# Attention, GLU and gate in one kernel: another order of the last two heads' query blocks, the first gate weights prepared among the projections, transposes two chunks at a time, and P times V at the end in twos

## The chip, the cores and the metric

The kernel runs on one core of a Trainium2 chip. A core has TensorE (PE in the profile, its weight loads PEld), VectorE (DVE), ScalarE (ACT), GpSimd (POOL) and SyncE (SP), each with an instruction queue that it works through in order, and 16 DMA engines. The metric is the device time of one execution in microseconds (us), the median of several runs. Before the change it is 2739.11 us (three runs, 2738.48 to 2739.22).

## The reference

With x of 2048 rows and 576 features, 32 heads of 18 features and a gate width of 4608:

```python
xn  = layernorm(x)
qkv = xn @ wqkv                                  # 576 -> 3 * 576
p   = softmax(q @ k^T * 18 ** -0.5)              # 32 heads, 2048 x 2048 each
s   = concat_heads(p @ v) @ wo
gate = xn @ W_gate;  gate = gate * (gate > 0)    # 576 -> 4608
h    = gate * (xn @ W_up)
g    = silu(h @ W_down)                          # 4608 -> 576
out  = x + s * g
```

Everything is float32.

## The kernel before

Almost every product is made of three float32r products: each operand is split into a rounded high part and the rest (low), and high x high, high x low and low x high are added up (`PRODUCTS`). `split_pool` (L96) makes such a pair on POOL, with a copy (L97) and a subtraction (L98); `split_full` (L89) makes one from PSUM, high on ACT (L90) and low on DVE (L91). All matmuls are issued at L64 and all transposes at L67, so the tile's name tells them apart.

**Projections.** The 2048 rows are taken in four groups g of 512. For each group `stats` and `normalize` work out the layernorm, and `transposed` turns the normalized rows into nine chunks of 64 features (`xs[g][c]`): four transposes into a PSUM bank (`tps`), then the split on ACT and DVE. For group 0 this is done ahead of all matmuls; for group g + 1 it is a generator (`rows_to_features`) that is fed into the matmuls of group g as `fill`: `row_pairs` issues the 54 matmuls of a block as 27 pairs (upper and lower 64 rows of the array at once) and takes one step of `fill` after every `every` pairs. `qk_block` makes 128 features of q and k at a time (four blocks, PSUM `pq`, then to DRAM as `qd`, `kd`), `qk_last` the rest, `v_block` makes v (PSUM `pv`, to DRAM as `vd`). In the last group the maxima for the first two heads (`pm`, reduced on DVE into `mx`, L189) are made among the matmuls of `v_block`.

**Units.** Then come 144 units, one for each of 36 slices of the gate width and four row groups. A unit k needs `gw`, the gate and up weights of its slice: `up_weights` loads them (`rg`) and splits them on POOL. It makes 54 matmuls (`pg`), relu and product (`h`, `hh`), and every second unit adds to `y` with 48 matmuls (`py`, `down`). Each unit begins by preparing the weights of unit k + 1; those of unit 0 are prepared by a call just before the first unit. Spread among the matmuls of units 9 to 143 lies the attention of 15 pairs of heads: scores (`psx`), exponentials on ACT (`p`, L640), P times V (`po`, `attend`), and the maxima of the next pair. The maxima reach the scores as extra rows of `qT`: `max_rows` works them out and writes them with eight small DMAs of SP (`qT<-nt`, L562) for two query blocks at a time. After the last slice of a row group `gate_steps` turns `y` into the silu factor, in pieces between matmuls: exponential on ACT (L508), plus one on DVE (L510), six reciprocals on DVE (L514), product on POOL (L515) and a store to `gd`.

**The end.** The 16th pair of heads (u = 15) is left for the end, with the output projection woven in. `exp_steps` with `last` takes the four query blocks of 512 in the order of `LASTQ`, each with 16 key tiles; two key tiles of both heads make one `p` tile and one `attend`. In the loop at the bottom each round issues four `psx`, takes at most one `attend`, and then about 2.2 us of matmuls from the generator `outputs`: the last `down`, then for each tile of 128 rows the output projection (`pw`) of its first 512 features (`first4`), whose heads come from DRAM (`od`, through `load_heads` and `heads`, tiles `o4`, `hf`), with the rows of `gd` and x (`rows_of`: `gt`, `xr`). The four tiles of `tail`, those of the last query block in `LASTQ`, get `first4` early and their last 64 features (`last1`, from `o5T`) at the very end. A query block is closed when `finish` has written its rows into `o5`. The weights `wo` are loaded and split on POOL when the units are over (`rw`, L739, L742).

What sets the order: the program's own text for matmuls, transposes and the operations marked `keep`; for the rest a scheduler that places each instruction on its engine's queue. SP issues nearly all loads, in its queue's order, and an SP entry that waits for a free buffer holds all behind it.

## Time and profile before

| | |
|---|---|
| median of three runs | 2739.11 us |
| the profiled execution's own time | 2731.45 us |
| its span, first to last instruction | 2729.7 us |
| PE busy | 2681.5 us (98%) |
| DVE, ACT, POOL busy | 1916.1, 1475.1, 1200.6 us |
| mean granted TensorE clock | 0.993 |
| 16 DMA engines | 92 GB/s over the span |

The page's parts on busy time tell that PE works nearly all the span; where it does not is seen in the views that list, for each instruction, how long its engine stood idle before it and what ended that (written in brackets as `[4.25 <-POOL gw L97]`, and summed in the view of waits). The view by stretches gives for each stretch its length, then for each engine its busy time and the number of instructions begun, then the granted TensorE clock (1.00 is full), the busy share of the DMA engines and the rate in GB/s. Rows of a timeline begin with the start and the length in us; a row can merge several instructions (`x4`). SPq and POOLq rows are DMAs being issued.

### The profile page before, as it was taken

How to read it: one execution, taken by the hardware profiler on the slowest of the kernel's cores; microseconds unless marked ns; L12 is line 12 of the kernel's file. 1: busy time of each engine (PE TensorE's matmuls, PEld its weight loads, DVE VectorE, ACT ScalarE, POOL GpSimd, SP SyncE). 2: the span in 40 equal slices, each digit the busy share in tenths (PEclk: the TensorE clock that was granted, in tenths of full speed). 3: DMA queues.
4: the chain of work that ended last, by engine and by line, in shares of the span. 5: the costliest groups of instructions: out<-in, count | busy, mean ns of one | idle time of the engine just before them, and what ended most of it. 6: DMA issues, size and time to landing. Idle time of an engine off the chain costs nothing.

```text
span 2729.7 us, 55255 instructions
## 1 busy us (share of the span) xinstructions
PE 2681.5 (98%) x22100; PEld 2013.2 (74%) x22100; DVE 1916.1 (70%) x3250; ACT 1475.1 (54%) x2686; POOL 1200.6 (44%) x929
## 2 busy tenths in 40 slices
PE   8998999999999999999999999999999999999898
PEld 6897777777777777777777777777777777777566
DVE  5426677777777777777777777777777777777452
ACT  3321356565656555555655555555556465656464
POOL 4225844444444444444444444444444444444322
PEclk9999999999999999999999999999999999999899
DMA  9744232232253222222342222222423222222244
GB/s 253 206 161 120 62 81 72 64 79 66 76 134 82 73 72 74 73 72 68 92 121 80 74 73 68 77 73 68 121 76 80 63 76 75 76 65 55 74 140 150
DMA packets 290368, 250.17 MB, mean 92 GB/s; under 512 B 60288, under 2 KB 232064, under 8 KB 290112
## 3 DMA queue, kind: packets, MB, share of 16 engines
q1 hardware_dynamic: 282048, 218.33, 30.5%
q0 software_dynamic: 8064, 28.32, 3.1%
q8 instruction: 175, 2.87, 0.4%
q14 instruction: 81, 0.66, 0.1%
HBM read 201.51 MB, written 44.53 MB: 90 GB/s over the span
## 4 chain that ended last, share of the span: by engine, by line
PE 94%; POOL 2%; ACT 1%; issue 1%; DVE 1%; DMA 1%; SPq 0%; DVEq 0%; POOLq 0%; ACTq 0%
PE pg L64 29%; PE py L64 17%; PE po L64 17%; PE pm L64 12%; PE psx L64 10%; PE pq L64 4%; PE pw L64 2%; PE pv L64 2%; PE tps L67 1%; PE tp L67 1%; POOL gw L98 0%; POOL y L491 0%; POOL dw L98 0%; ACT p L640 0%; DVE e L510 0%
## 5 line engine op out<-in xcount | busy, mean ns | idle before, releaser
L189 DVE TENSOR_REDUCE mx<-pm 128x1 f32<-128x512 f32 x2048 | 1359.4, 686 | 286.8 <-PE pm L64 167.2
L640 ACT ACTIVATE p<-psx 128x512 f32<-128x512 f32 x2048 | 1168.3, 598 | 576.0 <-PE psx L64 479.0
L64 PE MATMUL pg<-x,gw 64*128 64x512 f32 x7668 | 1370.6, 394 | 8.0 <-POOL gw L97 4.2
L64 PEld LDWEIGHTS pg<-x,gw 64*128 64x128 f32 x7668 | 1049.9, 186 | 125.2 <-POOL gw L97 4.6
L64 PE MATMUL psx<-qT,kT 56*128 56x512 f32 x2048 | 782.8, 399 | 14.3 <-DMA qT<-nt 10.5
L64 PE MATMUL pm<-kT,qT 54*128 54x512 f32 x2048 | 776.7, 405 | 0.3 <-ACT p L490 0.2
L64 PEld LDWEIGHTS py<-dw,hh 128*128 128x128 f32 x3456 | 461.8, 189 | 62.5 <-issue 61.3
L463 POOL TENSOR_TENSOR hh<-h,hh 128x512 fp32r<-128x512 f32 x144 | 184.7, 1282 | 733.5 <-ACT hh L462 690.8
L64 PE MATMUL py<-dw,hh 128*128 128x288 f32 x3456 | 480.0, 298 | 0.6 <-POOL hh L463 0.6
L64 PE MATMUL po<-p,va 128*32 128x512 f32 x4096 | 474.0, 596 | 0.0
L493 DVE TENSOR_TENSOR y<-py,y 128x288 f32<-128x288 f32 x520 | 237.9, 457 | 311.1 <-PE py L64 310.1
L64 PEld LDWEIGHTS pm<-kT,qT 54*128 54x128 f32 x2048 | 358.7, 185 | 121.1 <-issue 58.7
L64 PEld LDWEIGHTS psx<-qT,kT 56*128 56x128 f32 x2048 | 367.5, 186 | 62.3 <-DMA qT<-nt 11.3
L98 POOL TENSOR_TENSOR gw<-rg,gw 128x1152 fp32r<-128x1152 f32 x144 | 385.7, 2678 | 11.6
L64 PEld LDWEIGHTS po<-p,va 128*32 128x32 f32 x4096 | 115.8, 109 | 262.0 <-issue 256.5
L97 POOL CAST dw<-rd 128x576 fp32r<-128x576 f32 x144 | 95.6, 664 | 481.9 <-DMA rd<-in_B_W_down_dram 199.0
L98 POOL TENSOR_TENSOR dw<-rd,dw 128x576 fp32r<-128x576 f32 x144 | 205.8, 1429 | 11.6
L462 ACT ACTIVATE hh<-h 128x512 fp32r<-128x512 f32 x144 | 90.8, 630 | 169.3 <-DVE h L460 169.3
L97 POOL CAST gw<-rg 128x1152 fp32r<-128x1152 f32 x144 | 165.1, 1146 | 0.0
L64 PE MATMUL pq<-x,wqk 64*128 64x512 f32 x972 | 121.2, 397 | 0.0
L458 ACT ACTIVATE r<-pg 128x512 f32<-128x512 f32 x144 | 85.7, 595 | 63.2 <-PE pg L64 41.5
L556 ACT ACTIVATE nt<-tp 32x128 fp32r<-32x128 f32 x32 | 8.5, 266 | 193.3 <-PE tp L67 193.3
(88 smaller groups left out, 1203.3 us busy)
## 6 DMA issues: line engine op xcount, KB each, us to landing
rg<-in_B_W_gate_dram SPq DMA_DIRECT2D x144, 288.0 KB
rg<-in_B_W_up_dram SPq DMA_DIRECT2D x144, 288.0 KB
rd<-in_B_W_down_dram SPq DMA_DIRECT2D x144, 288.0 KB
x<-xTd SPq DMA_DIRECT2D x54, 256.0 KB
qT<-qd SPq DMA_DIRECT2D x384, 36.0 KB
kT<-kd SPq DMA_DIRECT2D x384, 36.0 KB
qd<-hh POOLq DMA_DIRECT2D x16, 512.0 KB, 4.0
kd<-hh POOLq DMA_DIRECT2D x16, 512.0 KB, 5.4
```

What stands on the lines that cost most here:

```text
L64: return tc.keep_in_program_order(nc.tensor.matmul(*args, **kw))
L67: return tc.keep_in_program_order(nc.tensor.transpose(*args))
L97: keep(nc.gpsimd.tensor_copy(hi, raw))
L98: keep(nc.gpsimd.tensor_tensor(lo, raw, hi.bitcast(F32), ALU.subtract))
L189: nc.vector.tensor_reduce(mx[:, g % 2, h, j, c : c + 1], ps, axis=AX.X, op=ALU.max)
L458: nc.scalar.activation(r, ps[0], AF.Relu)
L462: nc.scalar.activation(hh[:, 0], h, AF.Copy)
L463: keep(nc.gpsimd.tensor_tensor(hh[:, 1], h, hh[:, 0].bitcast(F32), ALU.subtract))
L493: nc.vector.tensor_tensor(ys[j][:, cs], ps, ys[j][:, cs], ALU.add)
L556: nc.scalar.activation(nt_.bitcast(F32R), ps[0:32, 0:P], AF.Copy)
L640: nc.scalar.activation(pts[key][:, h, i, :], ps, AF.Exp, scale=SCALE)
```

## The change

There are seven edits.

1. `transposed` yields after every second chunk instead of after each, and for groups 1 to 3 a step of `fill` is taken after every ninth pair of matmuls instead of every sixth.
2. For group 0 only the first four chunks (three steps) are transposed ahead of the matmuls; the others are taken in the first `qk_block`, a step after every sixth pair.
3. `up_weights(0)` is called after the last group's `qk_block`s and ahead of its `v_block`; `units`, `gus` and the function move up for that.
4. In `gate_steps` the addition of one goes from DVE to ACT.
5. `LASTQ` is (0, 3, 2, 1) instead of (3, 0, 2, 1): the query blocks counted from 1, in the order 1, 4, 3, 2.
6. In the loop at the bottom two `attend` are taken when three `p` tiles are ready, instead of one when two are.
7. The tail tiles' `gt` are kept in buffers of their own and not loaded again for the last step; their transposes from `o5` come after one row tile instead of two; of the last additions, those of tiles 0 and 2 are on POOL and those of 1 and 3 on DVE (before: 0 and 1 on POOL, 2 and 3 on DVE).

```diff
@@ -191,6 +191,19 @@
                         tasks.append((max_rows, ([qTs[u, g - 1], qT], mx)))
                     yield
 
+    units = [(g, f) for g in (NQ - 1, *range(NQ - 1)) for f in range(NF)]
+    gus = {}
+
+    def up_weights(k):
+        if k >= len(units):
+            return
+        f = units[k][1]
+        rg = wr.tile([P, KC, P], F32, name="rg")
+        load2(rg, [[(wg, f * P, P)], [(wu, f * P, P)]])
+        gw = ws.tile([P, 2, KC, P], F32R, name="gw")
+        split_pool(gw[:, 0], gw[:, 1], rg)
+        gus[k] = gw
+
 
     with ExitStack() as st:
         one = pool(st, "one", 1)
@@ -275,7 +288,8 @@
                 xs[g].append(xc)
                 if c % 3 == 0 and c + 3 < KC:
                     normalize(c + 3)
-                yield
+                if c % 2:
+                    yield
 
         def rows_to_features(g, xt):
             ln = []
@@ -304,10 +318,10 @@
                     fs = slice(f0, f0 + p1 - p0)
                     nc.gpsimd.dma_start(t[:, fs, gs].rearrange("i p s -> p i s"), hb[p0:p1])
 
-        def qk_block(b, gw, g, fill):
+        def qk_block(b, gw, g, fill, every):
             ps = next_pair("pq")
             row_pairs(
-                ps, lambda t, c, i, j, rows: (gw[rows, i, c, :], xs[g][c][rows, j, :]), fill
+                ps, lambda t, c, i, j, rows: (gw[rows, i, c, :], xs[g][c][rows, j, :]), fill, every
             )
             store_qk(b, ps, [(g, False), (g, False)])
 
@@ -360,8 +374,9 @@
             "wv", HC, [[[(wqkv, 2 * D + m * VH, VH)], [(wqkv, 2 * D + HC + m * VH, VH)]] for m in range(3)]
         )
         wqk.append(weights("wqk4", P, [[[(wqkv, C4, DT), (wqkv, D + C4, DT)]] * 2], pl=ws, tag="gw"))
-        for _ in transposed(0, *ln0):
-            pass
+        first = transposed(0, *ln0)
+        for _ in range(3):
+            next(first)
         for g in range(NQ):
             fill = None
             if g % 2:
@@ -376,7 +391,10 @@
             if g + 1 < NQ:
                 fill = rows_to_features(g + 1, nxt)
             for b in range(4):
-                qk_block(b, wqk[b], g, fill)
+                if b == 0 and g == 0:
+                    qk_block(b, wqk[b], g, first, 6)
+                else:
+                    qk_block(b, wqk[b], g, fill, 9)
                 if b == 0 and g == NQ - 1:
                     load_q(0, 0)
                     for c in range(NQ):
@@ -388,6 +406,8 @@
             if fill is not None:
                 for _ in fill:
                     pass
+            if g == NQ - 1:
+                up_weights(0)
             mx = [max_steps(0, h) for h in range(2)]
             v_block(wv, g, zip(*mx) if g == NQ - 1 else None)
 
@@ -398,20 +418,9 @@
     wl = pool(mid, "wl", 2, "right")
     yp = pool(mid, "yp", 8, "right")
 
-    units = [(g, f) for g in (NQ - 1, *range(NQ - 1)) for f in range(NF)]
-    gus, dws, hhs = {}, {}, {}
+    dws, hhs = {}, {}
     N1 = 9
     xcur = {NQ - 1: xs[NQ - 1]}
-
-    def up_weights(k):
-        if k >= len(units):
-            return
-        f = units[k][1]
-        rg = wr.tile([P, KC, P], F32, name="rg")
-        load2(rg, [[(wg, f * P, P)], [(wu, f * P, P)]])
-        gw = ws.tile([P, 2, KC, P], F32R, name="gw")
-        split_pool(gw[:, 0], gw[:, 1], rg)
-        gus[k] = gw
 
     def down_weights(k):
         f = units[k][1]
@@ -505,9 +514,9 @@
         while gates:
             y, t = gates.pop(0)
             e = wl.tile([P, D], F32, name="e", bufs=1)
-            tc.keep_in_program_order(nc.scalar.activation(e, y, AF.Exp, scale=-1.0))
+            keep(nc.scalar.activation(e, y, AF.Exp, scale=-1.0))
             yield
-            tc.keep_in_program_order(nc.vector.tensor_scalar(e, e, 1.0, None, op0=ALU.add))
+            keep(nc.scalar.activation(e, e, AF.Copy, bias=1.0))
             for n in range(6):
                 yield
                 cs = slice(n * GP, (n + 1) * GP)
@@ -617,7 +626,7 @@
 
     ready = []
     pts = {}
-    LASTQ = (3, 0, 2, 1)
+    LASTQ = (0, 3, 2, 1)
 
     def exp_steps(u, h, ppool, done, last=False):
 
@@ -708,7 +717,6 @@
             run_tasks()
 
 
-    up_weights(0)
     k = 0
     for n in (4,) + (5, 7) * 4:
         if 2 <= k < 2 + NQ:
@@ -776,8 +784,8 @@
         if i + 2 < NT:
             load_heads(horder[i + 2])
 
-    def rows_of(k):
-        gt = f2.tile([P, D], F32, name="gt")
+    def rows_of(k, pl=f2, name="gt"):
+        gt = pl.tile([P, D], F32, name=name)
         nc.sync.dma_start(gt, gd[k * P : (k + 1) * P, :])
         xt = f2.tile([P, D], F32, name="xr")
         nc.sync.dma_start(xt, x2[k * P : (k + 1) * P, :])
@@ -825,8 +833,9 @@
                 return 0.45
             return 0.0
 
+        gts = {}
         for k in tail:
-            gt, xt = rows_of(k)
+            gt, xt = rows_of(k, f1, f"gt{k}")
             t = parts[k] = f1.tile([P, D], F32, name=f"t{k}")
             hh = hq.pop(k)
             yield next_heads(k)
@@ -835,6 +844,7 @@
                 project(ps, first4(hh, cs))
                 nc.vector.tensor_tensor(t[:, cs], ps, gt[:, cs], ALU.mult)
                 yield 12 * 0.133
+            gts[k] = gt
             nc.gpsimd.tensor_tensor(t, t, xt, ALU.add)
             gate_out()
         end, since = None, 0
@@ -857,21 +867,20 @@
                 nc.sync.dma_start(out2[k * P : (k + 1) * P, :], xt)
                 if LASTQ[3] in closed and end is None:
                     since += 1
-                    if since == 2:
+                    if since == 1:
                         end = o5_rows(LASTQ[3])
-        gts = [rows_of(k)[0] if k < tail[3] else None for k in tail[:3]]
         while LASTQ[3] not in closed:
             yield 10.0
         o5T = end if end is not None else o5_rows(LASTQ[3])
         yield 0.45
         for j, k in enumerate(tail):
-            gt = gts[j] if j < 3 else rows_of(k)[0]
+            gt = gts[k]
             t = parts[k]
             for cs in halves:
                 ps = bank("pw")[:, :HC]
                 project(ps, last1(o5T, j, cs))
                 nc.vector.tensor_tensor(gt[:, cs], ps, gt[:, cs], ALU.mult)
-                (nc.vector if j > 1 else nc.gpsimd).tensor_tensor(t[:, cs], t[:, cs], gt[:, cs], ALU.add)
+                (nc.vector if j % 2 else nc.gpsimd).tensor_tensor(t[:, cs], t[:, cs], gt[:, cs], ALU.add)
                 yield 2 * 0.133
             nc.sync.dma_start(out2[k * P : (k + 1) * P, :], t)
 
@@ -886,7 +895,8 @@
     for n, _ in enumerate(zip(*[exp_steps(NU - 1, h, pp, done15, True) for h in range(2)])):
         if n % 2:
             run_tasks()
-            if len(ready) > 1:
+            if len(ready) > 2:
+                attend()
                 attend()
             due = min(due, 1.0) + 2.2
             while due > 0:
```

How this moves instructions is shown at three places. The first is PE's queue from the program's start, before (wqk_130 and the others are the weights of successive blocks):

```order
L67 MATMUL tps<-ident,xn 128x128 x36
L64 MATMUL pq<-x,wqk_130 128x512 x54
L64 MATMUL pq<-x,wqk_136 128x512 x36
L67 MATMUL tps<-ident,xn 128x128 x4
L64 MATMUL pq<-x,wqk_136 128x512 x12
L67 MATMUL tps<-ident,xn 128x128 x4
L64 MATMUL pq<-x,wqk_136 128x512 x6
```

and now:

```order
L67 MATMUL tps<-ident,xn 128x128 x16
L64 MATMUL pq<-x,wqk_130 128x512 x12
L67 MATMUL tps<-ident,xn 128x128 x8
L64 MATMUL pq<-x,wqk_130 128x512 x12
L67 MATMUL tps<-ident,xn 128x128 x8
L64 MATMUL pq<-x,wqk_130 128x512 x12
L67 MATMUL tps<-ident,xn 128x128 x4
L64 MATMUL pq<-x,wqk_130 128x512 x18
L64 MATMUL pq<-x,wqk_136 128x512 x54
L64 MATMUL pq<-x,wqk_144 128x512 x54
L64 MATMUL pq<-x,wqk_150 128x512 x18
L67 MATMUL tps<-ident,xn 128x128 x8
```

Group 0's last five chunks have moved into the first block, and group 1's transposes have moved two blocks later, where they come eight at a time (and 20 behind the fourth block).

The second place is POOL's queue from the last stores of q and k to the weights of unit 1 (vd stores of v, va the buffers for v, which are cleared once), before:

```order
L305 DMA kd<-hh 128x2x512
L337 DMA vd<-ev 128x8x72 x2
L536 MEMSET va_2950 128x832
L337 DMA vd<-ev 128x8x72 x2
L537 MEMSET va_2950 128x16
L538 MEMSET va_2950 128x16
L536 MEMSET va_2954 128x832
L537 MEMSET va_2954 128x16
L538 MEMSET va_2954 128x16
L97 CAST gw<-rg 128x1152
L98 TENSOR_TENSOR gw<-rg,gw 128x1152
L97 CAST gw<-rg 128x1152
```

and now:

```order
L319 DMA kd<-hh 128x2x512
L97 CAST gw<-rg 128x1152
L98 TENSOR_TENSOR gw<-rg,gw 128x1152
L351 DMA vd<-ev 128x8x72 x2
L545 MEMSET va_2956 128x832
L351 DMA vd<-ev 128x8x72 x2
L546 MEMSET va_2956 128x16
L547 MEMSET va_2956 128x16
L545 MEMSET va_2960 128x832
L546 MEMSET va_2960 128x16
L547 MEMSET va_2960 128x16
L97 CAST gw<-rg 128x1152
```

The two operations of unit 0's weights have moved ahead of the stores of v and the clearing of va; unit 1's weights are now the first to come behind these.

The third is PE's queue where the last unit is over and the 16th pair of heads begins (tp are transposes of the maxima and of the pair before), before:

```order
L67 MATMUL tp_34533<-ident,ot 128x128 x4
L64 MATMUL psx<-qT,kT_2324 128x512 x4
L64 MATMUL py<-dw,hh 128x288 x12
L64 MATMUL psx<-qT,kT_2324 128x512 x4
L64 MATMUL po<-p,va_2954 32x512 x4
L64 MATMUL py<-dw,hh 128x288 x6
L64 MATMUL psx<-qT,kT_2326 128x512 x4
L64 MATMUL po<-p,va_2954 32x512 x4
L64 MATMUL py<-dw,hh 128x288 x12
```

and now:

```order
L67 MATMUL tp_34533<-ident,ot 128x128 x4
L64 MATMUL psx<-qT,kT_2324 128x512 x4
L64 MATMUL py<-dw,hh 128x288 x12
L64 MATMUL psx<-qT,kT_2324 128x512 x4
L64 MATMUL py<-dw,hh 128x288 x6
L64 MATMUL psx<-qT,kT_2326 128x512 x4
L64 MATMUL po<-p,va_2960 32x512 x8
L64 MATMUL py<-dw,hh 128x288 x12
```

The po have moved back and come eight at a time (a po of the program is two instructions in the trace), and the qT of the first psx is now that of query block 0 instead of 3, which the rows do not tell. Between the first place and the third, from unit 0 on, PE's queue is the same but for buffer numbers.

## The prediction

> **What bounds the kernel now.** I read the page's busy times first, then the view of waits for PE, since an engine that is busy 98% of the span leaves time only where it stands.
>
> ```profile
> PE 2681.5 (98%) x22100; PEld 2013.2 (74%) x22100; DVE 1916.1 (70%) x3250; ACT 1475.1 (54%) x2686; POOL 1200.6 (44%) x929
> ...
> PE tps L67 <- ACT xn L260: 12.0, 2, 11.3
> PE psx L64 <- DMA qT<-nt: 10.5, 2, 10.2
> PE pg L64 <- POOL gw L97: 4.2, 1, 4.2
> PE psx L64 <- DVE mx L189: 2.9, 3, 1.0
> PE tps L67 <- DMA o<-od: 2.3, 1, 2.3
> PE pg L64 <- POOL gw L98: 1.5, 1, 1.5
> PE pw L64 <- DVE o5T L807: 1.4, 1, 1.4
> PE tps L67 <- ACT xn L263: 0.8, 1, 0.8
> ```
>
> Columns: total us, times, longest. PE stands for 48 us of the 2729.7, and the change touches what stands in most of these rows; the 144 units between are PE's work alone, and their order on PE stays. So I price each hole, and then what stands behind it. A hole costs more than its idle time. The view by stretches (last three columns: granted clock, DMA share, GB/s) shows it:
>
> ```profile
> 14.00:18.00 4.00, 3.21 (x16) 2.88 (x14) 3.85 (x8) 3.95 (x10) 2.65 (x1) 1.00 0.77 182
> 18.00:22.00 4.00, 4.00 (x33) 3.33 (x35) 3.71 (x9) 1.58 (x3) 3.12 (x2) 1.00 0.91 195
> 223.80:228.00 4.20, 2.71 (x12) 1.69 (x14) 0.00 (x0) 0.00 (x0) 4.08 (x3) 0.50 0.56 179
> 228.00:232.00 4.00, 4.00 (x22) 3.11 (x20) 1.38 (x2) 0.00 (x0) 2.28 (x1) 0.50 0.65 154
> 2573.70:2578.00 4.30, 3.83 (x12) 2.71 (x13) 0.08 (x1) 2.17 (x4) 1.40 (x1) 0.50 0.70 155
> 2578.00:2582.00 4.00, 4.00 (x22) 2.24 (x22) 0.83 (x2) 1.92 (x4) 0.00 (x0) 0.70 1.06 184
> ```
>
> After the two long holes the clock is 0.50 for some us: 22 matmuls in 4 us, against 33 at full clock, 0.121 us each.
>
> **The first gate weights (edit 3).** PE's, ACT's and POOL's timelines:
>
> ```profile
> 218.73 0.84 PE L64 MATMUL pm<-kT,qT 54*128 54x512 f32 x3
> 226.52 1.65 PE L64 MATMUL pg<-x,gw 64*128 64x512 f32 x6 [1.48 <-POOL gw L98]
> ...
> 235.82 0.60 ACT L458 ACTIVATE r<-pg 128x512 f32<-128x512 f32 x1 [16.18 <-PE pg L64]
> ...
> 219.08 0.79 POOL L536 MEMSET va<- 128x832 f32 x1 [7.05 <-PE pv L64]
> 222.62 1.14 POOL L97 CAST gw<-rg 128x1152 fp32r<-128x1152 f32 x1
> 223.84 2.62 POOL L98 TENSOR_TENSOR gw<-rg,gw 128x1152 fp32r<-128x1152 f32 x1
> ```
>
> PE ends the projections at 219.57 (218.73 + 0.84). POOL has idled 7.05 us for a buffer that v's matmuls free, clears it, and only then splits unit 0's weights. Unit 0 is 54 pg and 8 pm, 62 x 0.121 = 7.5 us, and its relu starts at 235.82: the hole costs 235.8 - 219.6 - 7.5 = 8.7 us, 5.7 idle and 3 of slow clock. Now both operations lie ahead of the stores of v, in POOL's idle time, and cost nothing there. Next late are unit 1's weights: they take the place of unit 0's behind the clearing and are done at 223.84 + 2.62 = 226.5; unit 0 would end at 219.6 + 7.5 = 227.1. The margin is 0.6 us. **-8.7**; bounds -9.5 and -2 (unit 1 waits a whole 3.8 us split, with a slow clock behind it).
>
> **The order 1, 4, 3, 2 (edit 5).** PE, then SP:
>
> ```profile
> 2562.96 0.66 PE L67 MATMUL tp<-ident,ot 128*128 128x128 f32 x4
> 2573.78 0.76 PE L64 MATMUL psx<-qT,kT 56*128 56x512 f32 x1 [10.16 <-DMA qT<-nt]
> 2597.01 0.67 PE L67 MATMUL tps<-ident,o 128*128 128x128 f32 x4 [2.34 <-DMA o<-od]
> ...
> 2570.68 3.16 SPq L562 DMA_DIRECT2D qT<-nt  x5
> 2580.47 0.42 SPq L783 DMA_DIRECT2D xr<-in_A_x_dram  x1
> 2594.26 10.71 SPq L765 DMA_DIRECT2D o<-od  x4
> ```
>
> The first scores wait for the maxima of block 4, whose small DMAs stand in SP's queue behind loads of wo. Block 1's were written with block 2's, in an earlier task; block 4's are then wanted a quarter of the tail later. Gone are 10.5 us of waiting (the row of waits) and the slow clock: half of 4.3 us and 0.3 of 4.0, 3.4. Against it: PE reaches the third head tile's transposes sooner. From 2573.78 to 2594.67 (2597.01 - 2.34) are 20.9 us; less 3.4, 0.4 of wait and 1.0 of po put off, 16.1 remain, so PE is there at 2563.6 + 16.1 = 2579.7. The load behind it needs SP, which is busy till 2580.9 (2580.47 + 0.42) with rows that don't move, and takes 2.75 us (2594.26 to 2597.01): PE waits till 2583.6, 3.9 us instead of 2.3, and its clock falls a little longer, 0.8 by estimate. -10.5 - 3.4 + 1.6 + 0.8 = **-11.5**; bounds -13.9 (no new wait) and -8.
>
> **P times V in twos (edit 6).**
>
> ```profile
> 2558.55 3.64 PE L64 MATMUL po<-p,va 128*32 128x512 f32 x32
> 2583.05 1.06 PE L64 MATMUL po<-p,va 128*32 128x512 f32 x8
> ...
> 2586.36 2.06 ACT L640 ACTIVATE p<-psx 128x512 f32<-128x512 f32 x4 [1.38 <-PE psx L64]
> ```
>
> 32 in a row take 0.114 each, 8 take 0.133: 0.15 a group, of which there are 16 fewer at most. No row shows groups of 16. 16 x 0.15 = 2.4; a group of 16 keeps part of it: **-1.8**, bounds -3.5 and 0. Four exponentials take 2.06 us in a round of some 3.7 of PE's, so ACT keeps up.
>
> **One added on ACT (edit 4).** DVE, POOL, and the nearest price of the added operation, the exponential over the same 128x576:
>
> ```profile
> 837.47 2.34 DVE L510 TENSOR_SCALAR e<-e 128x576 f32<-128x576 f32 x1
> 836.82 2.68 POOL L98 TENSOR_TENSOR gw<-rg,gw 128x1152 fp32r<-128x1152 f32 x1
> L508 ACT ACTIVATE e<-y x16: 675/684/730, 793.0 to 2618.6; 128x576 f32<-128x576 f32 x16
> ```
>
> L510 lasts until the subtraction on POOL ends (839.50), and the maxima behind it hold PE up: that is the row of 2.9 us in three times 1.0. It goes: -2.9. The addition costs ACT some 0.68, sixteen times; among the units ACT idles nearly half the time. In the tail four fall into a stretch where ACT is closer to full: +0.5, bounds 0 and 4 x 0.68 = 2.7. **-2.4**.
>
> **Transposes in twos, group 0 in the first block (edits 1, 2).** Between 14 and 18 us ACT (3.95 of 4) and DVE (3.85) are full and PE is not: matmuls put among the transposes start sooner, but the last chunk still comes out at ACT's pace near 20 us, and the last 18 matmuls behind it. I count 0.8 for the start, the 0.8 wait on xn L263 (group 1's transposes come two blocks later), and 0.4 for fewer changes between kinds: **-2.0**. Bounds: -5.2 (36 of the first block's matmuls hidden, 36 x 0.121, and that wait), and +2.4 (three waits of 0.8 in group 1's run of 20 transposes, which has two PSUM banks).
>
> **The last rows (edit 7).**
>
> ```profile
> 2711.40 5.58 PE pw L64 x42
> 2721.96 3.03 DMA gt<-gd
> ...
> 2720.00 3.05 POOL L874 TENSOR_TENSOR t<-t,gt 128x288 f32<-128x288 f32 x4 [0.99 <-DVE gt L873]
> 2725.85 0.82 DVE L874 TENSOR_TENSOR t<-t,gt 128x288 f32<-128x288 f32 x2
> 2561.34 1.24 DVE L552 TENSOR_TENSOR nx<-nm,nx 128x16 fp32r<-128x16 f32 x1 [0.68 <-ACT nx L551]
> 2561.28 1.27 POOL L463 TENSOR_TENSOR hh<-h,hh 128x512 fp32r<-128x512 f32 x1 [5.75 <-ACT hh L462]
> ```
>
> From 2711.40 to the last addition, 2726.67, are 15.3 us. Now: 5.6 of pw with 0.5 of transposes among them (ACT's and DVE's 1.3 us on o5T lie under the last 28), then DVE's 13 operations of 0.41 and 0.5 to the first: 11.9, so -3.4; the load of gt is gone. But tile 1's additions on DVE now fall beside tile 0's on POOL, tile 3's beside tile 2's, where DVE's today come behind POOL's. The L552 row is an addition of that kind on a tiny tile that ends with POOL's operation. Three of POOL's additions (3.05 / 4 each) waited out are +2.3. I lean to that: **-1.5**, bounds -4.7 and +1. [...]
>
> **Sum.** -8.7 - 11.5 - 1.8 - 2.4 - 2.0 - 1.5 = -27.9 us. It is made against the profiled execution of 2731.45 us (span 2729.7), which is 7.7 below the median of the runs; the holes are waits, which I take to be the same in both, so the median goes from 2739.1 to **2711**.
>
> **The rivals.**
>
> *The hole moves to unit 1.* The margin of 0.6 us is thin; if v's stores or the clearing run later, PE stands and its clock falls again: the term shrinks from -8.7 to -2, 2718. Against it: POOL's rows there have no wait but for PE. 0.12.
>
> *SP stays the bound at the end.* PE runs ahead into loads that SP issues at its old times: not one longer wait but two more of 2.5 us, and 1 us of slow clock: 2717. For it: the four o<-od issues at 2594.26 took 10.71 us. 0.12.
>
> *The change doesn't do what it says:* psx waits for the late DMAs although its block's came early, since they share queues: 11.5 is lost, 2722.7. The waits are per DMA, so 0.03.
>
> *A slow clock at the start.* The first matmuls now lie among transposes; were transposes not to count as work for the clock, these 36 would run at 0.50 as after the holes, 36 x 0.121 = 4.4 us more: 2715.6. Against it: from 18 to 22 us, right behind transposes alone, the clock is 1.00 and matmuls take 0.121. 0.05. [...]
>
> *Slower than before.* Taking two po groups at once makes PE stand for the second tile's exponentials: 16 pairs x 2.06 = 33 us, and the 1.8 gone: 2739.1 - 27.9 + 34.8 = 2746. It decides once more than 1.6 us a pair is exposed (26.1 / 16). Against it: the second tile's scores are a whole round, 3.7 us, ahead. 0.04.
>
> **How the numbers follow.** The forecast keeps 0.64, its own range 2704 to 2717. The bounds of the terms, seldom all on one side, and the rivals at 2715 to 2722 give **2702 to 2723** for 8 in 10. A measurement can tell about 0.2%, 5.5 us, from no change: all cases but the last lie below 2733.6. Faster 0.93, same 0.03 (several bounds at once), slower 0.04.
>
> **What would show it.** In the changed profile: no wait of pg on gw near 220 us, and clock 1.00 there; no wait of psx on qT<-nt, and a wait of tps on o<-od of 3 to 4 us; po in sixteens near 1.9 us; no wait of psx on mx; DVE's last additions longer than 0.45 beside POOL's; the end some 28 us sooner. Wrong it would be if units 9 to 143 took another time than before, or if a wait of pg on unit 1's gw or several on o<-od stood in the place of those removed.

## The result, and the profile after

The changed kernel takes 2707.76 us (median of four runs, 2705.44 to 2709.92) against 2738.8 us for the kernel before on the same chip (2731.39 to 2739.22): a ratio of 0.989, 95% interval 0.987 to 0.991. In one of three later comparisons, each on a chip of its own, the change ran again beside the kernel before: 2706.87 us (2705.72 to 2707.91) against 2732.36, ratio 0.9905 (0.9890 to 0.9919). The change itself hardly moves between the two (2705 to 2709 had been expected for the case that the scatter lies in the kernel before); it is the kernel before whose runs lie anywhere from 2731 to 2739. The two profiled executions, which are what the traces compare, differ by 23.3 us (2731.45 to 2708.17; spans 2729.7 to 2706.4).

The page's busy times of the changed kernel, then its view of waits for PE (total us, times, longest):

```profile
PE 2671.0 (99%) x22100; PEld 2016.1 (74%) x22100; DVE 1907.7 (70%) x3234; ACT 1480.5 (55%) x2702; POOL 1200.9 (44%) x929
...
PE tps L67 <- ACT xn L273: 11.5, 1, 11.5
PE tps L67 <- DMA o<-od: 5.6, 1, 5.6
PE tps L67 <- DVE x L91: 3.5, 3, 1.8
...
PE pw L64 <- DVE gt L882: 1.6, 3, 1.3
```

Gone are the waits on qT<-nt (10.5), on gw (4.2 and 1.5) and on mx (2.9). In their place stand a longer wait on o<-od (5.6 instead of 2.3), a new one on x (3.5) at the start and a slightly longer one on gt (1.6 instead of 1.3) at the end. The first row is the lead-in before the first transposes, which both kernels have.

PE's timeline of the changed kernel at the places the prediction speaks of, then POOL's beside the second of them:

```profile
41.59 1.85 PE L67 MATMUL tps<-ident,xn 128*128 128x128 f32 x8 [0.80 <-ACT xn L276]
...
52.97 1.26 PE L67 MATMUL tps<-ident,xn 128*128 128x128 f32 x8 [1.78 <-DVE x L91]
...
218.14 0.84 PE L64 MATMUL pm<-kT,qT 54*128 54x512 f32 x3
218.50 1.63 PE L64 MATMUL pg<-x,gw 64*128 64x512 f32 x10
226.58 0.50 PE L64 MATMUL pg<-x,gw 64*128 64x512 f32 x1 [0.44 <-ACT r L467]
2549.14 0.66 PE L67 MATMUL tp<-ident,ot 128*128 128x128 f32 x4
2572.59 1.09 PE L67 MATMUL tps<-ident,o 128*128 128x128 f32 x4 [5.63 <-DMA o<-od]
2573.33 3.23 PE L64 MATMUL pw<-wo,hf 128*128 128x288 f32 x12
2576.49 1.22 PE L64 MATMUL psx<-qT,kT 56*128 56x512 f32 x4
2579.49 1.86 PE L64 MATMUL pw<-wo,hf 128*128 128x288 f32 x12
2689.27 0.65 PE L67 MATMUL tp<-ident,ot 128*128 128x128 f32 x4 [0.80 <-ACT ot L578]
```

```profile
204.15 2.66 POOL L98 TENSOR_TENSOR gw<-rg,gw 128x1152 fp32r<-128x1152 f32 x1
...
223.27 2.67 POOL L98 TENSOR_TENSOR gw<-rg,gw 128x1152 fp32r<-128x1152 f32 x1
```

Unit 0's weights are done at 204.15 + 2.66 = 206.81 us, and its first pg follows the last maxima without a wait. Unit 1's are done at 223.27 + 2.67 = 225.94, and its first pg at 226.58 waits for something else, 0.44 us for r. Further down, the twelve pw behind the wait on o<-od take 3.23 us and, six us later, 1.86: the slow clock after a stop (granted 0.50 from 2570.87 to 2577.70 us).

**Where the 23.3 us went.** Five rows cut the execution into stages: the first pv of the last row group, unit 0's relu, the first transposes of ot, the last transposes of ot, and the end of the last addition. The table gives each stage's length in us, as differences of those rows' starts; the first column is the start of that pv. All kernels that were run are in it, since the stages are how the experiments below are read.

| kernel | to pv of group 3 | to relu of unit 0 | units | to last transposes of ot | to last addition |
|---|---|---|---|---|---|
| before | 200.09 | 35.73 | 2327.1 | 147.8 | 15.9 |
| the change | 199.48 | 26.45 | 2323.2 | 140.1 | 13.6 |
| the change, again | 199.80 | 26.49 | 2322.1 | 140.2 | 13.6 |
| edit 6 undone | 199.26 | 26.47 | 2323.4 | 138.6 | 13.4 |
| edit 5 undone | 198.26 | 26.48 | 2323.2 | 148.7 | 13.7 |
| edit 3 undone | 202.77 | 35.06 | 2322.5 | 140.0 | 13.7 |
| edits 1, 2 undone | 205.33 | 26.48 | 2324.0 | 140.1 | 13.7 |
| edit 4 undone | 196.52 | 26.49 | 2327.5 | 140.2 | 13.4 |
| heads three ahead | 204.20 | 26.49 | 2324.3 | 137.2 | 13.7 |
| additions shared as before | 199.19 | 26.47 | 2321.9 | 138.9 | 13.7 |
| group 1 one at a time | 198.56 | 26.50 | 2322.3 | 139.8 | 13.7 |
| heads three ahead, edit 6 undone | 199.63 | 26.46 | 2321.5 | 132.1 | 13.4 |
| all last additions on DVE | 201.68 | 26.48 | 2322.0 | 139.0 | 13.8 |
| these three (6, heads, group 1) | 195.72 | 26.47 | 2322.3 | 132.1 | 13.4 |

From before to the change the stages give -0.6, -9.3, -3.9, -7.7 and -2.3, together -23.8. Where kernels have the same code, a stage repeats within 0.1 us (second column), 2.7 (units), 1.3 (last transposes) and 0.3 (end); the first column wanders by 8 us with one and the same code. For the change run again no difference over 0.5 us was expected from the first unit to the end; the units differ by 1.1.

### The profile page after: what moved, and what is told of

Its sections match the earlier page's. It is cut to its first block, busy times and chain, and to the rows that moved or that the text cites. A ratio compares the mean times of both kernels' runs of the same rounds, so it can differ in the third digit from the quotient of the medians.

```text
span 2706.4 us, 55226 instructions
## 1 busy us (share of the span) xinstructions
PE 2671.0 (99%) x22100; PEld 2016.1 (74%) x22100; DVE 1907.7 (70%) x3234; ACT 1480.5 (55%) x2702; POOL 1200.9 (44%) x929
## 4 chain that ended last, share of the span: by engine, by line
PE 95%; POOL 2%; DVE 1%; DMA 1%; ACT 1%; issue 0%; SPq 0%; DVEq 0%; POOLq 0%; ACTq 0%
PE pg L64 29%; PE po L64 17%; PE py L64 17%; PE pm L64 12%; PE psx L64 10%; PE pq L64 4%; PE pw L64 2%; PE pv L64 2%; PE tps L67 1%; PE tp L67 1%; POOL y L500 1%; POOL gw L98 0%; DMA rgw<-in_A_wqkv_dram 0%; POOL hh L472 0%; DMA rd<-in_B_W_down_dram 0%
## 5 line engine op out<-in xcount | busy, mean ns | idle before, releaser
L98 POOL TENSOR_TENSOR gw<-rg,gw 128x1152 fp32r<-128x1152 f32 x144 | 385.6, 2678 | 11.5
```

The costliest lines, as they stand in the source:

```text
L98: keep(nc.gpsimd.tensor_tensor(lo, raw, hi.bitcast(F32), ALU.subtract))
```

## The experiments

Each kernel is the changed one with the edit that is shown. They were timed in three comparisons, each on a chip of its own with its own runs of the kernel before, whose medians were 2732.34, 2732.36 and 2732.95 us. The change itself ran in the second alone (with edit 4 undone, head tiles three ahead and the additions shared as before). Since the three medians lie within 0.6 us, all times are set beside its 2706.87.

### Edit 6 undone: P times V one group at a time

```diff
-            if len(ready) > 2:
-                attend()
+            if len(ready) > 1:
                 attend()
```

> The changed kernel with edit 6 undone alone: one attend a round as before. Theory (from the trace of the change): two attends in every second round leave rounds with neither po nor pw, in which PE has only four psx of 0.66 us and stands for ACT's four exponentials of 2.06 us; from the third head tile's transposes to the last tp the tail was 116.7 us against 113.7 before. So undone it is faster than the change by 2 to 3 us, that stretch some 114, about 2705 in the median. Rival (the prediction's term): po in sixteens saves 1.8 us, so undone it is 1.8 slower, the stretch 118 to 119.

Measured: 2706.23 us (2704.12 to 2707.39), ratio 0.9902 (0.9887 to 0.9917). In time that is no difference from the change. In the stage it is 138.6 us against 139.0 to 140.2 in the kernels that have the rest of this stage as in the change: 0.4 to 1.6 less, in one trace, where those scatter by 1.3 among themselves. So taking two groups at once gains nothing, and costs about 1 us as far as one trace can tell. The price of po fell, as foreseen (sixteen in 1.92 us, twice eight in 2 x 1.06). But the next round then has no po, and where it has no pw either, scores follow on scores. PE's and ACT's timelines of the change at one of three such places, then PE's of this kernel at its like:

```profile
2642.46 0.73 PE L64 MATMUL psx<-qT,kT 56*128 56x512 f32 x4
2643.12 0.66 PE L67 MATMUL tps<-ident,o 128*128 128x128 f32 x4
2643.71 1.89 PE L64 MATMUL psx<-qT,kT 56*128 56x512 f32 x4
...
2642.99 2.06 ACT L649 ACTIVATE p<-psx 128x512 f32<-128x512 f32 x4 [5.06 <-PE psx L64]
```

```profile
2627.14 0.73 PE L64 MATMUL psx<-qT,kT 56*128 56x512 f32 x4
```

With no po ahead of them the second four psx meet the exponentials of the first, still under way until 2645.05, and take 1.89 us instead of 0.73. From the third head tile's transposes to the last tp, counted from start to start, psx takes 21.9 us with pairs and 19.4 without, po 26.8 and 27.8; the whole of that stretch is 116.7 and 114.4 us, as the theory said. By these rows edit 6's own term was wrong in its sign.

### Edit 5 undone: the order 4, 1, 3, 2

```diff
-    LASTQ = (0, 3, 2, 1)
+    LASTQ = (3, 0, 2, 1)
```

> The changed kernel with edit 5 undone alone: query blocks 4, 1, 3, 2. Theory: psx waits 10 us for qT<-nt again with a slow clock behind it, and the wait of tps on o<-od falls from 5.6 to 2 to 3 us; from the first tp of the maxima to the third head tile's transposes 34 us instead of 23.5, so 10 to 11 us slower than the change, 2718. Rival: what the order gains is lost again to the heads' load, so only 5 us slower, 2713.

Measured: 2715.28 us (2714.5 to 2715.51), 8.4 more than the change; ratio 0.9935 (0.9919 to 0.9952). The stage is 8.5 to 9.7 us longer. PE's timeline of this kernel:

```profile
2558.78 0.76 PE L64 MATMUL psx<-qT,kT 56*128 56x512 f32 x1 [10.23 <-DMA qT<-nt]
...
2580.61 0.64 PE L67 MATMUL tps<-ident,o 128*128 128x128 f32 x4 [2.29 <-ACT e L517]
```

The wait on qT<-nt is back in full, and the one at the third head tile is short again (the row names ACT's e, which these transposes do not read; SP had started a load of o at 2577.82). The order is worth 9 us and not 11.5: it takes away 10.6 of waiting and some 2.6 of slow clock (behind that wait four psx take 1.9 us instead of 0.66, counted from start to start, and twelve py 3.1 instead of 1.8), and gives back 3.3 of waiting at the third head tile (5.63 - 2.3) and 0.8 of slow clock behind it: there tps, pw and psx take 1.09, 3.23 and 1.22 us in the change, and 0.64, 3.14 and 0.93 in this kernel.

### Edit 3 undone: unit 0's weights after the projections

```diff
-            if g == NQ - 1:
-                up_weights(0)
...
+    up_weights(0)
     k = 0
```

> The changed kernel with edit 3 undone alone: the weights of unit 0 are prepared just before the first unit. Theory: pg waits 5.7 us for gw again, and the clock is 0.50 for some 5 us behind it; unit 1's first matmul comes 9 us later than in the change, and the whole is 9 us slower, 2717. Rival (hole moved): the changed kernel pays part of it elsewhere, later units' weights being late, so undoing costs 5 or less, 2713.

Measured: 2717.68 us (2715.27 to 2719.18), 10.8 more than the change; ratio 0.9944 (0.9929 to 0.9959). PE's timeline of this kernel:

```profile
226.50 1.22 PE L64 MATMUL pg<-x,gw 64*128 64x512 f32 x4 [4.25 <-POOL gw L97]
229.20 1.22 PE L64 MATMUL pg<-x,gw 64*128 64x512 f32 x4 [1.48 <-POOL gw L98]
```

Both waits are back to the hundredth. From the pv to unit 0's relu it is 35.06 us against 26.46: the term is 8.6 us, where 8.7 was predicted. In the profiled execution the rest lies in the first column (202.77 us against 199.48 and 199.80), which wanders with one code as much as that.

### Edits 1 and 2 undone: transposes one at a time, group 0 ahead

```diff
-                if c % 2:
-                    yield
+                yield
...
-        first = transposed(0, *ln0)
-        for _ in range(3):
-            next(first)
+        for _ in transposed(0, *ln0):
+            pass
...
-                if b == 0 and g == 0:
-                    qk_block(b, wqk[b], g, first, 6)
-                else:
-                    qk_block(b, wqk[b], g, fill, 9)
+                qk_block(b, wqk[b], g, fill, 6)
```

> The changed kernel with edits 1 and 2 undone: a chunk at a time, a step after six pairs, all of group 0 ahead of the matmuls. Theory (from the trace of the change): they gain only 0.6 us at the end of the projections, since group 1's transposes now wait 4.2 us (on the layernorm and on two PSUM banks) and v's first matmuls start 2.8 us later, while groups 2 and 3 gain 1 to 2 us each; undone the projections end at 219 to 220 instead of 219.0, the median within 1 us of the change, 2708. Rival (the prediction): 2 us slower than the change, and the larger part of it in group 0.

Measured: 2712.44 us (2709.92 to 2718.22), ratio 0.9929 (0.9914 to 0.9943): slower than any expectation said, with four runs that spread over 8 us. Its profiled execution (2714.81 us) reaches the last pv at 205.33, 5.2 us later than the kernel before, though its transposes are the same. PE's timeline shows one stop that the kernel before does not have:

```profile
88.58 1.61 PE L67 MATMUL tps<-ident,xn 128*128 128x128 f32 x4 [3.49 <-ACT xn L276]
```

The granted clock is at half for 3.4 us behind it, and the first transposes begin 1.4 us later than before (12.69 and 11.26). So kernels with the same transposes can start 5 us apart. One piece is steady: from the pv of group 1 to that of group 2 it is 47.7 us in this kernel and before (106.92 to 154.61), and 45.3 in every kernel with the transposes in twos. That gain, 2.4 us, is in the code; what the first two groups do is taken up below.

### Edit 4 undone: the one added on DVE

```diff
-            keep(nc.scalar.activation(e, e, AF.Copy, bias=1.0))
+            keep(nc.vector.tensor_scalar(e, e, 1.0, None, op0=ALU.add))
```

> The change with edit 4 undone: the addition of one is on DVE again. Theory: it lasts until the subtraction on POOL ends (2.34 us instead of 0.45) and holds the maxima up; three waits of psx on mx of about 1.0 us come back, and the four additions of the tail leave ACT. +2.9 - 0.5 = +2.4 us over the change. Rival: the gain among the units had another source, since the change also shifts them by a few us; then no wait on mx and +0 us, the additions at 2.34 us all the same.

Measured: 2710.28 us (2709.62 to 2711.87), 3.4 more than the change; ratio 0.9918 (0.9903 to 0.9933). PE's view of waits of this kernel, then DVE's and POOL's timelines at one of the three places:

```profile
PE psx L64 <- DVE mx L189: 2.9, 3, 1.0
```

```profile
825.36 2.33 DVE L519 TENSOR_SCALAR e<-e 128x576 f32<-128x576 f32 x1
...
824.70 2.67 POOL L98 TENSOR_TENSOR gw<-rg,gw 128x1152 fp32r<-128x1152 f32 x1
```

The addition ends (827.69) a third of a microsecond after POOL's subtraction (827.37), and the three waits are back. The units take 2327.5 us against 2322.7 on average in the twelve executions with the addition on ACT: 4.8 us, where the three waits add up to 2.9. The rest lies behind each wait: set against the change run again, the units' relus lag by 1.4, 1.5 and 1.4 us more some units after the three places than ahead of them, and the granted clock is 1.00 all through. As I read it, PE then makes scores and maxima no faster than DVE, whose maxima have piled up, takes them (0.62 us each); no run takes that part by itself. And the tail has not become shorter without the four additions on ACT (140.2 us): the 0.5 us for ACT there was not to be seen.

### Head tiles three ahead

```diff
-        o4s[k] = hp.tile([P, 512], F32, tag="h", name="o4")
+        third = horder.index(k) % 3 == 2
+        o4s[k] = hp.tile([P, 512], F32, tag="r" if third else "h", name="o4", **(dict(bufs=1) if third else {}))
...
-        if i + 2 < NT:
-            load_heads(horder[i + 2])
+        if i + 3 < NT:
+            load_heads(horder[i + 3])
...
-    for k in horder[:2]:
+    for k in horder[:3]:
```

> The change, and the o4 tile of every third head tile in a buffer of its own, so that head tiles are loaded three ahead instead of two. Theory: the 5.6 us for which PE stands at the third head tile (tps on o<-od) are the price of a load that SP issues behind rows and too late; issued one head tile earlier, the wait goes, and with it the slow clock behind it (12 pw in 3.2 us instead of 1.6, four psx in 1.2 instead of 0.5): -5.6 - 1.5 = -7 us, between -5 and -8. Rival: SP or the DMA queues are the bound there (four o<-od issues took 10.7 us before), and the earlier load only pushes the rows behind it back: a wait of 3 us or more stays, at tps or at a row's gt, and the time is within 2 us of the change.

Measured: 2705.3 us (2700.79 to 2711.07), ratio 0.9900 (0.9885 to 0.9915): the time that the rival gave. Yet the wait on o<-od is gone (twelve transposes in one run, 1.67 us), and at the fifth head tile PE is 6.5 us earlier after the first transposes of ot than in the change, as foreseen. But the stage ends only 2.9 us shorter. Some 1.6 us are lost around exponentials that are still under way (PE waits 1.09 and 0.45 us on p), and 1.6 at another place, where PE's timelines of the change (run again) and of this kernel read:

```profile
2635.53 0.49 PE L64 MATMUL psx<-qT,kT 56*128 56x512 f32 x1 [0.72 <-DVE o5T L815]
2635.95 1.92 PE L64 MATMUL po<-p,va 128*32 128x512 f32 x16
```

```profile
2637.53 0.49 PE L64 MATMUL psx<-qT,kT 56*128 56x512 f32 x1 [0.72 <-DVE o5T L816]
2637.95 3.56 PE L64 MATMUL po<-p,va 128*32 128x512 f32 x16
```

and its view by stretches has there:

```profile
2638.00:2639.00 1.00, 1.00 (x9) 0.34 (x12) 0.20 (x1) 1.00 (x3) 0.00 (x0) 0.50 1.03 399
```

The same wait of 0.72 us, at the same instruction, is followed by po at full clock in one kernel and by 3.4 us at 0.50 (2637.89 to 2641.31) in the other. The last section sets the ten traces that have these scores side by side.

### The last additions shared as before

```diff
-                (nc.vector if j % 2 else nc.gpsimd).tensor_tensor(t[:, cs], t[:, cs], gt[:, cs], ALU.add)
+                (nc.vector if j > 1 else nc.gpsimd).tensor_tensor(t[:, cs], t[:, cs], gt[:, cs], ALU.add)
```

> The change with the last additions shared as before: tiles 0 and 1 on POOL, 2 and 3 on DVE. Theory: DVE's additions are slow only beside POOL's (1.50 us for two instead of 0.82); set behind POOL's they take 0.41 each, and from the last transposes of ot to the last addition, 13.6 us in the change, it takes 12.3 to 13.3. Rival: the sharing by turns is worth its price, because POOL with four additions in a row of 0.8 us ends last: 13.8 to 15. The whole time can hardly tell it (-1 to +1 us); the profile of the tail can.

Measured: 2707.61 us (2704.99 to 2707.82), ratio 0.9908 (0.9891 to 0.9924). The end takes 13.7 us, as in the change: neither expectation, and the theory's number is missed. POOL and DVE of this kernel:

```profile
2695.13 3.28 POOL L883 TENSOR_TENSOR t<-t,gt 128x288 f32<-128x288 f32 x4
...
2696.79 1.94 DVE L883 TENSOR_TENSOR t<-t,gt 128x288 f32<-128x288 f32 x2
2699.39 0.81 DVE L883 TENSOR_TENSOR t<-t,gt 128x288 f32<-128x288 f32 x2
```

DVE's first two additions fall beside POOL's four after all, and end 0.3 us after them (2698.73 and 2698.41). The next two, with POOL idle, take 0.81.

### All last additions on DVE

```diff
-                (nc.vector if j % 2 else nc.gpsimd).tensor_tensor(t[:, cs], t[:, cs], gt[:, cs], ALU.add)
+                nc.vector.tensor_tensor(t[:, cs], t[:, cs], gt[:, cs], ALU.add)
```

> The change with all eight last additions on DVE and none on POOL. Theory: an addition on DVE is slow only beside POOL's; alone, each takes 0.41 us (0.82 for two), in every place, and 16 operations of 0.4 us end at the same time as now: 13.4 to 14 us from the last transposes of ot to the last addition, the time within 1 us of the change. Rival: the first additions of DVE are slow for a reason of their own (0.75 us each here too): 14.5 to 15.5.

Measured: 2707.39 us (2705.3 to 2707.77), ratio 0.9902 (0.9888 to 0.9917); the end takes 13.8 us. DVE and POOL:

```profile
2697.32 1.24 DVE L883 TENSOR_TENSOR t<-t,gt 128x288 f32<-128x288 f32 x2
2699.21 0.81 DVE L883 TENSOR_TENSOR t<-t,gt 128x288 f32<-128x288 f32 x2
...
2696.46 1.42 POOL L866 TENSOR_TENSOR xr<-xr,gt 128x576 f32<-128x576 f32 x1 [2.72 <-DVE gt L864]
```

The first two still stretch, beside an addition of POOL on another tile; from 2697.88, when POOL has ended for good, every pair takes 0.81. So here DVE's additions are slow beside POOL's even when that is on another tile (1.24 us for two, 0.81 alone), as the theory has it; its "in every place" fails where POOL is still at work. This also shows why three ways of sharing end alike. Sixteen operations of 0.4 us on DVE are 6.5 us; giving POOL some of them costs DVE about what it saves.

### Group 1's transposes one at a time

```diff
-                if c % 2:
+                if c % 2 or g == 1:
...
-                    qk_block(b, wqk[b], g, fill, 9)
+                    qk_block(b, wqk[b], g, fill, 9 if g else 6)
```

> The change, but group 1's transposes alone go one chunk at a time at every sixth pair again, as all did before; group 0's stay in the first block and groups 2 and 3 in twos at every ninth. Theory: what edits 1 and 2 gain lies in group 2 (2.4 us less in the profiles), and in group 1 they lose 2 to 3: its transposes have lost the first block, two chunks at a time outrun xn and the two PSUM banks, and PE stands 3 to 5 us there. With the old step group 0 ends at 53 to 54.5 us instead of 53.2 to 59.9, and the time is 1.5 to 3 us below the change (2704 to 2705.5 where the change has 2706.9). Rival: the stops there come from the rows, which arrive late in some executions, and no step of the transposes helps: group 0 ends at 55 to 60 us here too and the time is that of the change.

Measured: 2706.62 us (2704.46 to 2708.87), ratio 0.9902 (0.9885 to 0.9918): the time of the change, so the theory's time is missed. In the profile the waits on x fall from 2.8 or 3.5 us to 1.44, but one on xn of 2.44 stands, as the rival has it. Behind that one are DVE and POOL:

```profile
34.27 1.62 DVE L254 TENSOR_TENSOR ln<-ln 128x4 f32<-128x4 f32 x1
...
33.84 2.03 POOL L98 TENSOR_TENSOR wv<-rgw,wv 128x864 fp32r<-128x864 f32 x1
```

An addition over four numbers a row takes 1.62 us and ends at 35.89, POOL's subtraction at 35.87. In the changed kernel it is another of these small steps:

```profile
38.10 2.48 DVE L257 TENSOR_TENSOR ln<-ln,ln 128x4 f32<-128x4 f32 x1
...
38.51 2.04 POOL L98 TENSOR_TENSOR wv<-rgw,wv 128x864 fp32r<-128x864 f32 x1
```

(40.58 and 40.55.) Some of POOL's splits wait for their weights to land (in this kernel 1.82 us, till 29.88; in the change 0.81, till 33.21), so which of the steps of the layernorm fall beside a split, and how long xn is late, differs between the two executions. This is one source of the wandering of the first column, seen in two traces. Two more can be read off the traces: the first transposes begin anywhere from 11.0 to 12.7 us, and behind the waits on xn and x the granted clock is at half, ahead of the last pv for 3.4 us in the change, 13.7 in "Head tiles three ahead" and not at all in "The three together" (199.48, 204.20 and 195.72 us in the first column). That these are all of it is not shown, nor that the 7 us between runs of the kernel before come from there, since none of its executions at 2739 us left a trace.

### Head tiles three ahead, P times V one at a time

The edits of "Head tiles three ahead" and "Edit 6 undone" together.

> The change with head tiles loaded three ahead and P times V one group at a time. With both groups at once, the earlier loads took 6.5 us out of the profile before the third head tile, and 3.6 came back behind it: PE stood for the exponentials of the second tile, and one slow clock of 1.6 us. Theory: groups one at a time leave an exponential a round more, so that nothing of the first comes back: from the first transposes of ot to the last, 138.6 us with single groups alone, now 132 to 133.5, and the time is 6 to 8 us below the change (2699 to 2701 where that has 2706.9). Rival: the stops behind the third head tile are those of a tail in which ACT is full (it also has the gates' added one now), however the groups are taken: 135.5 to 138, and 2702 to 2705.

Measured: 2699.66 us (2698.64 to 2702.34), ratio 0.9877 (0.9862 to 0.9892), 7.2 less than the change. PE's timeline of this kernel:

```profile
2547.62 0.66 PE L67 MATMUL tp<-ident,ot 128*128 128x128 f32 x4
2565.18 1.53 PE L67 MATMUL tps<-ident,o 128*128 128x128 f32 x12
2679.73 0.66 PE L67 MATMUL tp<-ident,ot 128*128 128x128 f32 x4 [0.80 <-ACT ot L578]
```

2679.73 - 2547.62 = 132.1 us, at the short end of the theory's 132 to 133.5: with groups one at a time the 6.5 us stay (138.6 to 132.1). With groups in twos 2.9 of them were left. So edit 6 costs about a microsecond where it stands, and more of what another edit brings; but 1.6 of the 5.1 us between 137.2 and 132.1 are the one slow clock, which the other traces with that stop lack.

### The three together

> The two before the last together: head tiles three ahead, P times V one group at a time, and group 1's transposes one at a time. If their gains lie in different places they add up: 8 to 10.5 us below the change, 2696.5 to 2699 where that has 2706.9. If the start's is given back later (POOL and DVE set the pace of the units), 2699 to 2701.

Measured: 2700.54 us (2695.48 to 2701.65), ratio 0.9875 (0.9860 to 0.9890). The two that shorten the tail give their 132.1 us here too; group 1's transposes add nothing that the runs can tell. The time is that of the second case, but not for its reason: in the profile the units take 2322.3 us, as elsewhere, so nothing is given back there. The version that beats both kernels is the one before this, the change without edit 6 and with head tiles three ahead; the two can't be told apart in time.

## Why the prediction was right, and where not

The forecast was 2711 us with a range of 2702 to 2723; it came out at 2707.76. That it is so near is in part luck, two errors that cancel. The sum was -27.9 from the profiled execution; the profiles moved by -23.3. And the 7.7 us between the profiled execution and the median of the kernel before, which the prediction took to be common to both, did not carry over: the change's profiled execution lies 0.4 us above its median.

- **The first gate weights, -8.7.** Right: 9.3 between the two profiles, 8.6 by undoing it. Unit 1's weights had the margin of 0.6 us that was worked out (225.94, and the first pg at 226.58 waits for r), so the hole did not move to unit 1.
- **The order 1, 4, 3, 2, -11.5.** The mechanism was right in all its parts: the wait on qT<-nt goes, a longer one on o<-od comes. Mis-sized was that new wait: 5.63 us instead of 3.9. The clock behind it costs 2.3 us (pw 3.23 - 1.86, psx 1.22 - 0.73, tps 1.09 - 0.66), of which 1.5 lay behind the shorter wait too, so the 0.8 more that was estimated is right. The slow clock that goes, 3.4 in the sum, is 2.6 by the rows of the kernel with edit 5 undone. The step that failed is that the load takes 2.75 us from its start on SP. SP's timeline of the change shows it starting 1.5 us after the transposes that free its buffer (they end at 2566.96; till 2568.41 it issues a row of gt and one of x, which the prediction took not to move), and 4.1 pass from there to the data; the view by stretches has the DMA engines full just then:

```profile
2568.51 0.86 SPq L773 DMA_DIRECT2D o<-od  x2
```

```profile
2567.00:2570.00 3.00, 0.00 (x0) 0.00 (x0) 1.29 (x3) 2.93 (x6) 0.00 (x0) 1.00 1.18 198
2570.00:2572.60 2.60, 0.01 (x1) 0.04 (x1) 2.60 (x5) 0.00 (x0) 0.00 (x0) 0.67 0.97 335
2572.60:2574.00 1.40, 1.40 (x7) 1.40 (x8) 1.21 (x2) 0.23 (x1) 0.06 (x1) 0.50 0.94 361
```

  The measured worth is 9 us. With a buffer more the load goes ahead of all this and the wait is gone, so the rival that SP stays the bound at the end falls: one wait, not several, and the buffer sets it.
- **P times V in twos, -1.8.** Wrong: about +1 us. The step that failed is "ACT keeps up": it was reckoned for the mean round (2.06 us of exponentials in 3.7 of PE's), but in twos the rounds are unequal, and in the short ones ACT is late. The rival of the exponentials had the right place; its price of 33 us was some twenty times what the exposed scores cost (2.5 us of psx, less 1.0 of po).
- **One added on ACT, -2.4.** Right in kind, half in size: 4.4 to 4.8. The wait was priced by its idle time alone; behind it PE loses about half as much again, as I read it to DVE's backlog, and the 0.5 for ACT in the tail did not come.
- **Transposes, -2.0.** Not to be settled in size. Of its parts, the 0.8 us wait on xn is still there (41.59), and the 0.8 for the start did not come in the execution compared: from the first transposes to the end of the first block's matmuls it is 14.45 us before, 14.59 in the change, and 13.6 to 14.6 in all with edit 2. Group 2's 2.4 us are steady (0.4 was counted for fewer changes between kinds); in the first two groups PE waits 3 to 5 us on xn and x, the runs of transposes on two PSUM banks that the bound of +2.4 was made for. Undoing both edits cost 5.6 us in the runs, but its profile holds a stop of 3.49 us that the kernel before, with the same transposes, lacks, and with one code the start stage lies anywhere from 196 to 204 us.
- **The last rows, -1.5.** Right, with the waiting on POOL's additions that was leaned to: the end went from 15.9 to 13.6 us, -2.3. The new sharing of the additions has no part in it that the traces can tell, since with the old one it is 13.7; the rest of the edit is left as the cause, and was not undone by itself. DVE and POOL of the changed kernel:

```profile
2698.52 1.50 DVE L883 TENSOR_TENSOR t<-t,gt 128x288 f32<-128x288 f32 x2
2702.09 0.82 DVE L883 TENSOR_TENSOR t<-t,gt 128x288 f32<-128x288 f32 x2
...
2697.94 1.77 POOL L883 TENSOR_TENSOR t<-t,gt 128x288 f32<-128x288 f32 x2
```

  Two additions beside POOL's take 1.50 us, two alone 0.82.
- **A slow clock at the start** did come, in both kernels, and not for the rival's reason. The view by stretches gives 1.00 there, but the traces hold no record of the granted clock ahead of 16.99 us (before) and 17.70 (the change), and a stretch without a record counts as 1.00. PE's timelines, of the kernel before and then of the change, show it:

```profile
11.26 5.96 PE L67 MATMUL tps<-ident,xn 128*128 128x128 f32 x27 [11.26 <-ACT xn L260]
18.00 1.21 PE L67 MATMUL tps<-ident,xn 128*128 128x128 f32 x9 [0.79 <-ACT xn L260]
```

```profile
15.19 2.79 PE L64 MATMUL pq<-x,wqk 64*128 64x512 f32 x12
18.94 1.66 PE L64 MATMUL pq<-x,wqk 64*128 64x512 f32 x12
```

  Before, the slow stretch lies on the first 27 transposes (0.22 us each, the next nine 0.13), and the full clock follows 5.7 us of transposes alone. So the rival's condition was not met in that run: transposes alone were followed by the full clock. In the change 12 of the 36 matmuls fall into the slow stretch and take 1.1 us more, not the 4.4 of the rival; the transposes that are no longer in it gain about as much.

By stages the terms that were measured give -9 (edit 3), -4.6 (4), -9 (5), +1 (6), -2.3 (7), and -0.6 for edits 1 and 2 in the two executions compared: -24.5, against -23.8 by the stages of the two profiles. The rival of a change that doesn't do what it says falls with the wait on qT<-nt, and the one on the slower side with the times.

## What to carry to other kernels

Price a wait not by its idle time but by what stands behind it: here 2.9 us of waiting cost 4.4 to 4.8, by my reading through another engine's backlog, and 5.6 cost 7.9 through the clock. When work is grouped to save changes of kind, reckon the engine that feeds it in the shortest round, not in the mean one. And when a wait is taken away, look for the next load whose buffer is freed only by the work that now comes sooner: one more buffer for it brought 6.5 us here.

## What the runs showed of the hardware

- DVE's additions over 128x4 took 1.62 and 2.48 us beside POOL's subtractions instead of 0.16, and ended 0.02 and 0.03 us after them. In the fourteen traces 414 additions and products of DVE on two SBUF tiles start while an operation of POOL runs (its DMA issues apart), and all 414 end after that operation; 210 of them, additions over 128x16 (nx) beside POOL's product hh, take 1.24 to 1.26 us and end 0.03 to 0.04 after it, where those with POOL idle take 0.16 or 0.17. (The one of 2.48 us began 0.41 ahead of POOL's subtraction; what held it until then is not shown.) The prediction had this for the last additions and one row of 1.24 us, not as what makes the start wander.
- Stops of PE of the same length were followed by a slow clock in one trace and not in others: four scores spread over 2.5 us, with a stop of 0.72 among them, PE's longest there, stand in ten of the fourteen traces, and in "Head tiles three ahead" alone are they followed by 3.4 us at half clock. Within each trace the changes of the granted clock lie whole multiples of 3.41 us apart (in the change at 17.70, 55.25, 58.66, 2570.87, 2577.70 and 2700.58 us, which are 11, 1, 736, 2 and 36 steps; 2512.21 / 736 = 3.413). Laid on the grid of these steps, the 2.5 us fall into one step but for 0.06 us in the trace that lost its clock; in the other nine at least 0.3 us fall into a second one. Whether the place on the grid is what decides is not shown: no run was made to move a stop along it.
